# A rebuilt instruction order for a two-kind attention kernel: measured durations of the residual sums and of dependent ScalarE waits put into the planner

## The chip, the cores and the metric

The kernel runs on one core of a Trainium2 chip. The metric is the device time of one execution in microseconds (us), a median over several executions. "DVE" is VectorE, "ACT" ScalarE, "PE" TensorE, "SP" the SyncE sequencer that issues the DMAs.

## The reference

Four layers in a row on x of shape 1 x 2048 x 512 in bf16, with 32 heads of 16 columns: A, B, A, B. Cut to what matters:

```python
def _A_ref(x, wqkv, w_phi, wo):        # linear attention with softmax features
    q, k, v = heads(x @ wqkv)
    phi_q = concat(softmax(q @ w_phi), softmax(-(q @ w_phi)))
    phi_k = concat(softmax(k @ w_phi), softmax(-(k @ w_phi)))
    kv = einsum("bhsf,bhsd->bhfd", phi_k, v)          # a sum over the whole sequence
    z  = einsum("bhsf->bhf", phi_k)
    return (phi_q @ kv) / (phi_q @ z + 1e-6)  @ wo
def _B_ref(x, wqkv, wo):               # sliding window: 8 positions, 2 apart
    ...                                # softmax(q . k[s - 2w]) @ v[s - 2w], then @ wo
for L in range(2):
    x = x + _A_ref(layernorm(x), ...)
    x = x + _B_ref(layernorm(x), ...)
```

The sequence is cut into four blocks of 512 positions. The sums `kv` of a layer A need all four blocks: behind them stands a joint where nothing of that layer's second half can have begun. In what follows joint 0 and joint 1 are the two moments at which the masking operation on the transposed sums (output tile ZM) starts on DVE.

## The kernel before

Each piece of work is a closure in a thread (stage and engine). One string gives the order in which the threads are stepped, one gives each free choice DVE or ACT, one gives buffers. The instructions of every engine, SP included, are issued in the order of the string.

```python
def flex(self, stage, fn, *args):                 # work that DVE or ACT may do
    k = self.nflex; self.nflex += 1
    self.step(stage, "F%d%s" % (k, fn.__name__), fn, *args, _CHOICE[k] == "1")
def run(self):
    self.setup(); self.stages()
    for w in _ORDER.split():                      # 1452 entries
        key = self.names[int(w, 36)]
        i = n.get(key, 0); n[key] = i + 1
        self.threads[key][i]()
```

In layer B the values are copied to 32 partitions for each of four shifts: `vrep`, four DMAs of 131.5 KB each, from the tile V into the tile Vg.

```python
def rdb(s):                                       # "broadcast reload"
    T["P", s] = pr = self.med([4, NB, P], "Prho")
    a = rd[0:1, s, 0:P]
    src = bass.AP(a.tensor, a.offset, [[2 * pitch, 8], [0, 16], [1, 16 * P]])
    nc.sync.dma_start(out=pr[:]..., in_=src)      # DRAM -> SBUF, rows of 4096 bytes
def muld(s):
    nc.vector.tensor_tensor(out=ev[:], in0=ev[:], in1=T["P", s][:], op=ALU.mult)
def vrep(dl):                                     # "value loads"
    ...
    for g in (0, 2, 1, 3):
        a = T["V"][dl:dl + 1, 0:1, 2 + 2 * g:3 + 2 * g]
        src = bass.AP(a.tensor, a.offset, [[4 * a.ap[0][0], H], [1, VGW]])
        nc.sync.dma_start(out=self.Vg[L, b][dl // 2][32 * g:32 * g + 32, dl % 2, 0:VGW], in_=src)
                                                  # SBUF -> SBUF, rows of 4208 bytes
```

## Time and profile before

| | before |
|---|---|
| time, median of 3 | 328.98 us (328.91 to 330.25) |
| span in the profile | 327.5 us |
| busy PE / DVE / ACT | 310.3 / 302.2 / 279.3 us |
| joint 0, joint 1 | 53.70, 209.28 us |
| joint 0 to joint 1 | 155.58 us |
| joint 1 to the end of the last DVE instruction | 113.63 us |
| from there to the end of the span | 4.59 us |

The last three lines are differences of the two joints, of the end of the last DVE instruction (322.91 us) and of the span.

The granted clock is the share of its full speed at which PE was allowed to run.

### The profile page before, as it was taken

What the parts mean: (1) busy time and instruction counts of PE and PEld (TensorE: products, weight loads), DVE (VectorE), ACT (ScalarE), POOL (GpSimd) and SP (SyncE); (2) the same over time, 40 slices, a digit from 0 to 9 for tenths busy, and PEclk for the clock granted to TensorE, in tenths of its full rate; (3) what the DMA queues carried; (4) which work ended last, traced back from release to release, by engine and by line L of the source; (5) the groups of instructions that cost most, each with busy time, mean ns of one, the idle gap of its engine ahead of it and who ended that gap; (6) DMA issues with size and microseconds to landing.
All of it is one profiled execution on the core that took longest, in us unless ns stands there. A gap on an engine that the chain in (4) does not pass through costs nothing. (4 is left out here: it accounts for less than half of the span.)

```text
span 327.5 us, 8033 instructions
## 1 busy us (share of the span) xinstructions
PE 310.3 (95%) x3176; PEld 149.5 (46%) x3203; DVE 302.2 (92%) x439; ACT 279.3 (85%) x634; POOL 25.3 (8%) x50
## 2 busy tenths in 40 slices
PE   7999999999999999999999999979999999999873
PEld 3655456445444444443444455644544454433221
DVE  7998995998998999899999999699999999999993
ACT  5999988998888999989999999798999996676550
POOL 4000000000021003000000000000000208400000
PEclk9999999999999999999999999999999999999999
DMA  7980000004556899998750300023436977679952
GB/s 197 380 197 3 0 2 4 2 20 120 105 148 135 152 164 133 139 121 154 137 135 1 67 3 2 4 59 90 128 58 125 179 146 134 150 139 158 166 176 92
DMA packets 37388, 35.41 MB, mean 108 GB/s; under 512 B 23008, under 2 KB 32224, under 8 KB 37344
## 3 DMA queue, kind: packets, MB, share of 16 engines
q1 hardware_dynamic: 36816, 34.81, 53.6%
q8 instruction: 27, 0.44, 0.6%
q14 instruction: 17, 0.14, 0.2%
q10 hardware_dynamic: 528, 0.02, 0.1%
HBM read 10.50 MB, written 2.36 MB: 39 GB/s over the span
## 5 line engine op out<-in xcount | busy, mean ns | idle before, releaser
L927 PE MATMUL ps<-xnT,WB 128*128 128x512 bf16 x384 | 87.6, 380 | 0.5 <-DMA xnT<-xn 0.5
L1081 DVE TENSOR_TENSOR pav<-PT,Vg 128x4096 bf16<-128x4096 bf16 (+1 forms) x34 | 72.0, 2162 | 1.5 <-DMA Vg<-V 1.0
L1019 DVE TENSOR_TENSOR prod<-QT,K 128x4096 bf16<-128x4096 bf16 x32 | 72.5, 2291 | 0.3 <-ACT QT L192 0.2
L927 PEld LDWEIGHTS <-WB 128*128 128x128 bf16 x384 | 42.3, 114 | 43.3 <-issue 5.8
L520 PEld LDWEIGHTS <-oT 128*128 128x128 bf16 x256 | 23.8, 97 | 34.5 <-ACT oT L192 5.7
L192 ACT CAST oT<-ps 128x512 bf16<-128x512 f32 (+1 forms) x60 | 32.1, 587 | 8.4 <-PE ps L1090 7.1
L706 ACT ACTIVATE Eq<-ps 128x512 bf16<-128x512 f32 x64 | 34.0, 615 | 0.7 <-PE ps L698 0.6
L520 PE MATMUL ps<-WoB,oT 128*128 128x512 bf16 x122 | 32.1, 380 | 2.4 <-ACT oT L192 2.0
L599 ACT ACTIVATE Ek<-ps 128x512 bf16<-128x512 f32 x64 | 33.6, 622 | 0.4 <-PE ps L593 0.2
L698 PE MATMUL ps<-xnT,WA 128*128 128x512 bf16 x128 | 30.7, 380 | 0.6 <-DVE Eq L816 0.6
L540 ACT ACTIVATE sqd<-x 128x512 bf16<-128x512 bf16 x48 | 30.1, 643 | 1.0 <-DVE x L533 0.8
L605 PE MATMUL ps<-WA,xnT 128*128 128x512 bf16 x120 | 30.0, 380 | 0.5 <-issue 0.2
L593 PE MATMUL ps<-WA,xnT 128*128 128x512 bf16 x124 | 29.7, 380 | 0.6 <-DMA xnT<-xn 0.2
L520 PE MATMUL ps<-WoA,oT 128*128 128x512 bf16 x120 | 29.2, 380 | 0.4
L533 DVE SCALAR_TENSOR_TENSOR x<-ps,x 128x512 bf16<-128x512 f32 x38 | 25.4, 686 | 1.9 <-PE ps L520 1.7
L192 ACT CAST V<-ps 128x512 bf16<-128x512 f32 x31 | 17.5, 595 | 4.4 <-PE ps L927 4.3
L192 ACT CAST K<-ps 128x512 bf16<-128x512 f32 x31 | 17.8, 585 | 3.7 <-PE ps L927 3.3
L530 ACT ACTIVATE x<-ps 128x512 bf16<-128x512 f32 x26 | 15.1, 598 | 6.4 <-PE ps L523 6.3
L192 ACT CAST QT<-ps 128x512 bf16<-128x512 f32 x29 | 17.1, 592 | 2.5 <-PE ps L927 2.5
L651 DVE TENSOR_TENSOR Ek<-Ek,rk 128x4096 bf16<-128x4096 bf16 (+1 forms) x10 | 18.6, 1858 | 0.5 <-ACT rk L646 0.5
L593 PEld LDWEIGHTS <-xnT 128*128 128x128 bf16 x128 | 12.1, 97 | 15.4 <-DMA xnT<-xn 0.7
L446 ACT ACTIVATE xn<-x,nmr,rstd 128x512 bf16<-128x512 bf16 x23 | 18.2, 822 | 1.0 <-DVE nmr L435 0.8
(129 smaller groups left out, 433.3 us busy)
## 6 DMA issues: line engine op xcount, KB each, us to landing
Vg<-V SPq DMA_DIRECT2D x128, 131.5 KB, 4.4
Prho<-rd SPq DMA_DIRECT2D x8, 512.0 KB
x<-in_A_x_dram SPq DMA_DIRECT2D x3, 512.0 KB
WB<-in_B_wqkv_dram SPq DMA_DIRECT2D x3, 512.0 KB, 11.6
wraw<-in_A_wqkv_dram SPq DMA_DIRECT2D x4, 256.0 KB, 4.5
out_dram<-x SPq DMA_DIRECT2D x4, 256.0 KB, 2.2
out_dram<-x SPq DMA_DIRECT2D x8, 128.0 KB, 2.2
x<-in_A_x_dram SPq DMA_DIRECT2D x4, 128.0 KB
```

What stands on the lines that cost most here:

```text
L192: self.nc.scalar.copy(out=out, in_=in_)
L520: nc.tensor.matmul(y[:], lhsT=oT[:, c, t * P:(t + 1) * P], rhs=Wo()[:, c, :], start=(c == 0), stop=(c == NB - 1 and not onpe))
L533: nc.vector.scalar_tensor_tensor(out=xb[:, t, :], in0=T[t][:], scalar=1.0, in1=xb[:, t, :], op0=ALU.mult, op1=ALU.add, **kw)
L540: nc.scalar.activation(out=sqd[:], in_=xb[:, t, :], func=ACT.Square, accum_out=T["ss"][:, t:t + 1])
L593: nc.tensor.matmul(pk[:], lhsT=xnT[:, t, k, :], rhs=self.WA[:, k, D:2 * D], start=(k == 0), stop=(k == NB - 1))
L599: nc.scalar.activation(out=T["E"][:, t, s, :], in_=T["k", t][:], func=ACT.Exp, scale=1.0 - 2.0 * s)
L605: nc.tensor.matmul(pv[:], lhsT=xnT[:, t, k, :], rhs=self.WA[:, k, 2 * D:3 * D], start=(k == 0), stop=(k == NB - 1))
L698: nc.tensor.matmul(pq[:], lhsT=self.WA[:, k, hb * P:(hb + 1) * P], rhs=xnT[:, :, k, :], start=(k == 0), stop=(k == NB - 1))
L706: nc.scalar.activation(out=self.Eq[L, b][s][:, :, hb, :], in_=T[hb][:].rearrange("p (t i) -> p t i", t=4), func=ACT.Exp, scale=1.0 - 2.0 * s)
L927: nc.tensor.matmul(pp[:], lhsT=self.WB[:, k, i * D + c:(i + 1) * D:NB], rhs=xnT[:, :, k, :], start=(k == 0), stop=(k == NB - 1))
L1019: nc.vector.tensor_tensor(out=pr[:], in0=QT[:, c:c + 1, :].to_broadcast([P, NW, TB]), in1=win, op=ALU.mult)
L1081: nc.vector.tensor_tensor(out=pv, in0=PT[:, :, lo:lo + n].unsqueeze(1).to_broadcast([P, NB, 2, n]), in1=vw, op=ALU.mult)
```

## The change

The planner that made the order string had its durations of residual sums on DVE and of waits between dependent ACT instructions replaced by measured ones, and built all strings anew: 1452 order entries, 383 choices (68 flipped), all buffer slots. Nothing is computed otherwise; options that were switched off are deleted.

```diff
-    "half_k": ((0, 3), (1, 3)),
+    "half_k": {(0, 3): 1, (1, 3): 1},        # the same two halves for the same two blocks
-    "v_dram": (),                            # was off
-    "rho_pad": 0,                            # was off
 _ORDER = """                                 # 1452 entries, cut
-...
+...
 _CHOICE = (                                  # the first of four lines
-    "0011111111111001110111111010000010010000000000000001011111101100100000110101000110000010000001110111"
+    "1111111111110110111111111010000000001000000001000101001011100100000000110011100010000000000010110100"
 ...
 _SLOTS = {                                   # cut
```

Decoded, the part of the order string that came to matter is that of SP in the first pair of layers (block number in brackets):

```
before: rdb 1 (3) | vrep 0 (0), vrep 0 (1) | tr (2) | vrep 1, 2, 3 (1) | tr (3) | vrep 1, 2, 3 (0)
after:  rdb 1 (3) | vrep 0, 1 (0) | tr (2) | vrep 0, 1, 2, 3 (1)       | tr (3) | vrep 2, 3 (0)
```

## The prediction

> **What bounds the kernel now.** I read four views in this order: busy time by engine, the timeline of slices, a table of windows cut at the two layer joints and at the tail, and the chain of waits. First the page's busy line and its slices.
>
> ```profile
> PE 310.3 (95%) x3176; PEld 149.5 (46%) x3203; DVE 302.2 (92%) x439; ACT 279.3 (85%) x634; POOL 25.3 (8%) x50
> PE   7999999999999999999999999979999999999873
> DVE  7998995998998999899999999699999999999993
> ACT  5999988998888999989999999798999996676550
> ```
>
> Three engines are nearly full at once. TensorE is idle for 327.5 - 310.3 = 17.2 us, VectorE for 25.3, ScalarE for 48.2. A new order does not shorten any instruction; it can only close idle time, so these are all there is to win. VectorE shows two dips, at slice 7 and at slice 26: the joints where the key-value sums of the first-kind layer are complete, are transposed and masked (I call them joint 0, at 53.7 us, and joint 1, at 209.28 us) and everything behind them must start anew. The windows, cut there and where the last VectorE products begin:
>
> ```profile
> 0.00:53.70 53.70, 51.62 (x588) 28.70 (x594) 47.73 (x105) 47.08 (x99) 5.12 (x30) 1.00 0.41 119
> 53.70:209.28 155.58, 152.88 (x1597) 72.89 (x1609) 145.28 (x202) 144.44 (x337) 7.27 (x11) 1.00 0.53 92
> 209.28:240.00 30.72, 28.34 (x424) 14.51 (x428) 28.03 (x69) 27.58 (x75) 0.00 (x0) 1.00 0.27 74
> 240.00:295.12 55.12, 53.95 (x396) 25.26 (x396) 54.34 (x40) 46.15 (x97) 12.91 (x9) 1.00 0.76 139
> 295.12:322.91 27.79, 23.50 (x175) 8.12 (x177) 26.81 (x27) 14.06 (x30) 0.00 (x0) 1.00 0.81 161
> 322.91:327.50 4.59, 0.00 (x0) 0.00 (x0) 0.00 (x0) 0.00 (x0) 0.00 (x0) 0.88 0.22 70
> ```
>
> The columns are the window, its length, then busy time of PE, weight loads, DVE, ACT and POOL, then the granted clock, the DMA share and GB/s. Idle per window, PE / DVE: 2.1 / 6.0 up to joint 0; 2.7 / 10.3 between the joints; 2.4 / 2.7 behind joint 1; 1.2 / 0.8 from 240 to 295; 4.3 / 1.0 in the tail; then 4.6 us in which nothing computes and the last store lands. So TensorE is the bound between the joints (98% busy), and VectorE is the bound from joint 1 to the end: 109.18 us of its work in 113.63 us. The clock is full, so nothing is lost there.
>
> The chain of waits agrees where it can be followed (it breaks off at 219 us): long PE stretches in the projection, then PE waiting for a VectorE product, then short hops.
>
> ```profile
> 266.65 7.77 PE ps L927 x36
> ...
> 292.91 2.30 DVE prod L1019
> 295.21 0.04 issue
> 295.25 0.61 PE ps L1026 x8
> ...
> 315.27 1.00 PE ps L1090 x16
> 316.27 0.00 issue
> 316.28 1.58 ACT oT L192 x3
> 317.86 0.05 issue
> 317.90 0.39 PE ps L520
> ```
>
> 36 matmuls in 7.77 us is 0.216 us each: at full stream. At 295.25 TensorE waits 1.2 us (its largest wait after the start) for the last product; behind that it feeds on what VectorE hands out.
>
> [...]the 384 projection matmuls of L927 have a mean duration of 380 ns but cover 87.6 us together, and 384 x 0.216 = 82.9 us; so 4.7 us of small stalls hide inside "busy". [...]2.29 us for 4096 bf16 elements of SBUF, 0.68 us for 512 of PSUM. So moving small work between engines is an exchange of known prices. [...]behind joint 1 the logarithm of a small tile and the exponential that reads its result start 0.43 us apart (211.00 and 211.43), the full length of the first; the next instruction, which depends on neither, starts 0.21 us after (211.64).
>
> **The change part by part.** The half_k table says the same as before (two halves for the same two blocks), and the DRAM route and pad that are deleted were switched off. Left are three strings: the order, the engine choices and the buffer slots. The lists have equal length (1452 order entries, 383 choices), so every result is computed as before.
>
> Choices: 68 of 383 flip, and they nearly cancel. Prices are mean durations from the groups by form.
> - Layer-norm applications: net 7 go to VectorE (3 in the first norm, 4 behind the first-kind layers), 4 leave it behind the second-kind layers: net +3 x 0.408 = +1.22 us VectorE, -3 x 0.822 = -2.47 ScalarE.
> - PSUM copies of 512 columns: net +1 to VectorE, plus one of 256 columns (taken as 0.42): +0.69 + 0.42; ScalarE -0.59 - 0.37. One weight copy of 1024 columns goes the other way: -0.69 and +1.01.
> - Residual sums: net 2 leave VectorE, one with its accumulator read (0.686 + 0.083) and one without: -1.46; ScalarE +0.598 + 0.204 + 0.598 = +1.40, and TensorE must add x by two more identity matmuls: +2 x 0.216 = +0.43.
> - The broadcast products: 25 direct ones become 23; each change saves VectorE 0.682 - 0.416 = 0.27 and costs a ScalarE copy of 0.589: -0.53 and +1.18.
> Sum: VectorE -0.35, ScalarE +0.16, TensorE +0.43 us. Nothing here is worth a tenth of a per cent. Behind joint 1, where VectorE is the bound, I counted the same list: -0.07 us. So the VectorE-bound last third keeps its 109 us of work; it can gain only from its 4.45 us of idle time.
>
> Order: joint 0 stands behind the same TensorE entry, joint 1 too, and from the third product of block 2 in the last layer on, the next 18 VectorE entries (products and weighted values, some 34 us of work) are the same in both. Changed in detail: the copy at joint 0 goes from VectorE (0.69) to ScalarE (0.59), 0.1 us on a serial path; at joint 1 one query projection moves between the denominators, so that TensorE has work while the reciprocal is made; five instead of three broadcast products there go through a ScalarE copy, which frees PSUM sooner; in the tail, the last copy goes to VectorE and one residual to ScalarE, which puts three instead of four 0.69 us sums behind the last product but adds a 0.42 us copy ahead of them.
>
> What each stretch may give, as a judgement: about a third of its bound engine's idle time, since both orders are products of the same kind of search and much of the idle time is the shape of the graph.
> - up to joint 0: PE idle 2.1, of which 1.27 precedes the first matmul: 0.4 us;
> - between the joints: PE idle 2.7 and perhaps 2.5 of the hidden stalls: 1.6 us;
> - joint 1 to 240 us: VectorE idle 2.7: 0.9 us;
> - from there to the end: VectorE idle 1.8: 0.5 us; the landing of the last store stays.
> That is 3.4, less about 0.2 for the extra matmuls (half of 0.43, as one falls in the tail where TensorE has room): 3.2 us. 328.98 - 3.2 = 325.8 us.
>
> **The rivals.**
> - Full benefit. If the better prices let the order fit the chip, most idle time goes. The floor for TensorE is 310.3 + 0.43 + 1.27 of start + 5.3 behind its last matmul = 317.3 us of span. Getting half way there from 327.5 gives 322.4, a little over 323 us timed. For it: dependent ScalarE pairs are many (some 50 logarithm-exponential pairs) and the old order may have counted them short. Against: ScalarE has 48 us to spare, so its error was mostly absorbed.
> - No benefit. The waits only change places: TensorE between the joints is at 98%, VectorE behind joint 1 at 96%. Then the time is 328 to 329 us.
> - A new wait. In the new order of the DMA queue the first store of block 0's result stands between the value loads of blocks 3 and 2 of the last layer; before, all value loads came first. If the residual is late, the queue holds those loads, and VectorE waits as it did once before (1.0 us at 135.51, for a value load). With rotated buffers and some TensorE waits for PSUM this could cost 1 to 2 us: 330 to 331. Against: the blocked block is the last one used, many products later.
>
> **Range and chances.** The middle estimate is 325.8 us. The third I assumed could be a tenth (328) or two thirds (322.5). The range of 322.4 to 328.7 us should hold it 8 times in 10. Faster by over 2% needs less than 322.4 us, that is 6.6 of about 10 recoverable us: 0.09. Slower by over 2% means 335.6 or more, for which no work was added: 0.02. Within 2%: 0.89.
>
> **What would show it.** Busy time of all three engines should move by less than 1 us each; if VectorE falls by several, my price list is wrong. VectorE's idle time should shrink from 25.3 to 21 to 23 us, TensorE's from 17.2 to about 13 to 15. Joint 1 should come near 207.5 us instead of 209.28, and the stretch from it to the last VectorE instruction should be near 112.3 instead of 113.6. If joint 1 comes at the same time and the gain is all behind it, the step on the TensorE-bound middle was wrong; if a wait for a value load or for PSUM over 1 us appears in VectorE's or TensorE's waits, the third rival is at work. The prediction fails if the time is outside the range, above all if one of the joints turns out to have been a stall of several us that the windows hide.

The 2.29 and 0.68 us are the two-tensor products of DVE in the trace of before (L1019, both operands in SBUF; L816, one in PSUM). The logarithm that starts at 211.00 us lasts 0.40 us there.

## More of the kernel before

In blocks 2 and 3 of layer A the factor rho (one over the denominator) is written to DRAM and read back to be spread over partitions: `rdb`, twice per block, 512 KB each, into tile Prho. `muld` multiplies by it on DVE.

`tr` transposes the normed input of the next layer (xnT).

The prediction shows the busy lines and a table of windows. One line of the page that it does not show is the clock granted to PE in 40 slices, in tenths:

```profile
PEclk9999999999999999999999999999999999999999
```

A 9 is 90% or more, so no slice lost a tenth of it. The trace has one stretch at half clock, from 326.42 us on, behind the end of compute.

## The result, and the profile after

The changed kernel takes 334.37 us (median of 4, 333.08 to 334.77) against 328.95 us for the kernel before in the same series. The ratio is 1.0151, with a 95% interval of 1.0112 to 1.0190. Such a ratio here is always the mean time of one kernel's fast runs over that of the other's of the same rounds, so it is not quite the ratio of the medians. In the whole study one run was slow (336.90 us, of e8_before_value_traffic); it is left out of the ratios. The change is within 2%, but on the other side of 1 than predicted, and outside the range.

These lines are from the changed kernel's page: busy time, then the slices of PE, of DVE and of the granted clock.

```profile
PE 313.4 (94%) x3179; PEld 150.2 (45%) x3205; DVE 302.0 (91%) x440; ACT 280.0 (84%) x635; POOL 21.2 (6%) x50
PE   8999999999997999999999999979999999999782
DVE  8899995998968799999999999698999999999992
PEclk9999999999997999999999999997999999999998
```

DVE and ACT do the same work as before; PE has 3.1 us more, though only three matmul records more. DVE has a new 6 in slice 12 (91.5 to 99.8 us), PE a 7 in slice 13, and the clock, without a dip before, has a 7 in slice 13 and one in slice 28. The table of windows of the changed kernel, cut at its own joints and at the places that answer to those of before (columns: window, length, busy PE, weight loads, DVE, ACT, POOL, granted clock, DMA share, GB/s):

```profile
54.53:212.77 158.24, 154.07 (x1598) 73.63 (x1609) 144.44 (x200) 145.97 (x340) 6.53 (x12) 0.99 0.50 90
212.77:240.00 27.23, 24.34 (x402) 11.71 (x406) 23.98 (x56) 23.59 (x59) 0.00 (x0) 0.94 0.31 83
240.00:298.58 58.58, 58.42 (x408) 27.98 (x412) 57.81 (x53) 49.95 (x113) 9.54 (x9) 1.00 0.73 127
327.44:332.69 5.25, 0.00 (x0) 0.00 (x0) 0.00 (x0) 0.00 (x0) 0.00 (x0) 0.83 0.27 87
```

So the span grew by 5.2 us in four places: joint 0 comes 0.83 later (54.53 for 53.70), the stretch between the joints is 2.66 longer (158.24 for 155.58), the one behind joint 1 is 1.04 longer (327.44 - 212.77 = 114.67 for 113.63), and the end without compute 0.66 (5.25 for 4.59). Joint 0 needs no cause in the order: the later profiles with full clock at the start have it at 53.41 to 54.61 with the changed beginning and at 53.80 to 54.70 with the old one. The other three differences repeat.

**The new wait at 100 us.** The timeline of the kernel before, SP's DMA issues (columns: start, us from first to last issue of the group, what, count):

```profile
87.06 3.03 SPq L451 DMA_TRANSPOSE xnT<-xn  x1
90.19 0.60 SPq L831 DMA_DIRECT2D Prho<-rd  x1
95.28 6.79 SPq L988 DMA_DIRECT2D Vg<-V  x8
```

and of the kernel after:

```profile
86.67 2.87 SPq L448 DMA_TRANSPOSE xnT<-xn  x1
90.10 0.59 SPq L828 DMA_DIRECT2D Prho<-rd  x1
90.80 9.96 SPq L976 DMA_DIRECT2D Vg<-V  x8
102.76 2.42 SPq L448 DMA_TRANSPOSE xnT<-xn  x1
```

The second reload of block 3 is issued at the same time in both. Before, the next eight DMAs (value loads) follow at 95.28, when it is nearly through. In the new order ACT makes V of block 0 earlier (its last copy ends at 87.73 us instead of 95.20), so SP need not wait for it, and they stand right behind the reload, at 90.80. The old order kept the two apart only by chance: its loads waited for V, which came when the reload was nearly through. The DMA records of the trace show what this does to the reload's 4096-byte packets (counted per us, with the mean time of one):

```
            before                    after
93 us   28 of 277 ns              18 of 471 ns  and 16 value packets of 398 ns
94 us   30 of 281 ns              17 of 501 ns  and 16 value packets of 491 ns
95 us   the last 10, of 261 ns    16 of 535 ns  and 16 value packets of 508 ns
97 us   -                         16 of 498 ns  and 16 value packets of 516 ns
98 us   -                         the last 2
```

About half as many packets, each about twice as long (471 to 535 ns for 261 to 281), and from 92 to 97 us the DMA share of the windows view is 1.04 of the core's 16 engines where it was 0.41. The product that needs the reload, in the timeline of the kernel before:

```profile
96.03 2.39 DVE L835 TENSOR_TENSOR Eq<-Eq,Prho 128x2048 bf16<-128x2048 bf16 x2
100.14 0.65 PE L900 MATMUL ps<-Eq,R 32*32 32x512 bf16 x32
```

and after (in square brackets: idle time just before, and what ended it):

```profile
98.59 0.43 PE L897 MATMUL ps<-Eq,R 32*32 32x512 bf16 x16
100.30 1.23 DVE L832 TENSOR_TENSOR Eq<-Eq,Prho 128x2048 bf16<-128x2048 bf16 x1 [2.91 <-DMA Prho<-rd]
101.58 0.44 PE L897 MATMUL ps<-Eq,R 32*32 32x512 bf16 x16 [2.55 <-DVE Eq L832]
```

DVE waits 2.91 us for the reload, and PE, which holds the second half of the matmuls that read Eq at the head of its queue, 2.55 us for DVE.

**The half clock.** From 102.24 us, PE runs for 3.41 us at half clock. In the windows view of the changed kernel the second line has the granted clock 0.61 (third number from the end):

```profile
98.00:101.58 3.58, 1.03 (x21) 0.26 (x19) 1.28 (x2) 0.97 (x3) 0.00 (x0) 1.00 0.54 108
101.58:106.00 4.42, 4.42 (x27) 1.72 (x27) 4.38 (x6) 3.72 (x7) 0.29 (x1) 0.61 0.78 150
```

In that stretch, matmuls of 512 columns start 0.427 us apart, for 0.216 us elsewhere. The three half-clock stretches of this execution start at 102.24, 225.12 and 330.93 us, the first two last 3.413 us each, and the later two start 122.88 and 228.69 us behind the first: 36 and 67 times 3.4133 us. The two starts ahead of the end of compute lie 36 such lengths apart in after_again too (100.2 and 223.1 us) and 26 in e4_block1_first (224.1 and 312.8). In the 3.41 us ahead of the first stretch PE was busy for 0.25 of the time (0.86 us), ahead of the second for 0.64 (2.17 us). That share alone does not tell: from 310.46 to 313.87 us PE was busy for 0.46 of the time, and the clock stayed at 1.00 behind it. These shares take PE's busy time from the trace, whose matmul ends are modelled. The second stretch lies behind joint 1; there PE does many small matmuls of 32 rows or columns between waits of 0.2 to 0.6 us. The third lies behind the end of compute and costs nothing.

**The end.** The last DVE instruction and the last four stores in the timeline of the kernel before:

```profile
322.22 0.69 DVE L533 SCALAR_TENSOR_TENSOR x<-ps,x 128x512 bf16<-128x512 f32 x1 [0.35 <-PE ps L520]
320.62 3.10 SPq L544 DMA_DIRECT2D out_dram<-x  x4
```

and after:

```profile
326.75 0.69 DVE L530 SCALAR_TENSOR_TENSOR x<-ps,x 128x512 bf16<-128x512 f32 x1 [0.43 <-PE ps L517]
325.74 3.54 SPq L541 DMA_DIRECT2D out_dram<-x  x4
```

The issue of the last store is through at 323.72 before, 0.81 us behind the end of that DVE instruction, and at 329.28 after, 1.84 us behind it. In the new order the last store but one, which stores a residual made on ACT, is in issue from 327.23 to 328.81 us, and the last store stands behind it; before, the last store but one took 0.33 us. This repeats: 0.79 to 1.60 us in the seven other executions with the new second part, 0.33 us in all six with the old one.

### The profile page after: what moved, and what is told of

It is laid out like the page before. It is cut to its first block, busy times and chain, and to the rows that moved or that the text cites. A ratio compares the mean times of both kernels' runs of the same rounds, so it can differ in the third digit from the quotient of the medians.

```text
span 332.7 us, 8019 instructions
## 1 busy us (share of the span) xinstructions
PE 313.4 (94%) x3179; PEld 150.2 (45%) x3205; DVE 302.0 (91%) x440; ACT 280.0 (84%) x635; POOL 21.2 (6%) x50
## 4 chain that ended last, share of the span: by engine, by line
PE 74%; ACT 10%; DMA 9%; DVE 4%; issue 1%; SPq 1%; DVEq 0%; ACTq 0%
PE ps L924 24%; PE ps L517 12%; PE ps L590 7%; PE ps L602 7%; DMA Vg<-V 6%; PE ps L695 5%; PE ps L1012 4%; PE ps L1076 4%; ACT Eq L703 3%; DMA Prho<-rd 3%; PE ps L665 2%; PE ps L285 2%; PE ps L457 1%; DVE pav L1067 1%; PE ps L897 1%
## 5 line engine op out<-in xcount | busy, mean ns | idle before, releaser
L924 PE MATMUL ps<-xnT,WB 128*128 128x512 bf16 x384 | 89.0, 385 | 0.0
L190 ACT CAST oT<-ps 128x512 bf16<-128x512 f32 (+1 forms) x56 | 30.0, 585 | 8.5 <-PE ps L1076 6.5
L517 PE MATMUL ps<-WoA,oT 128*128 128x512 bf16 x120 | 31.4, 392 | 0.6 <-DVE oT L188 0.2
L590 PE MATMUL ps<-WA,xnT 128*128 128x512 bf16 x123 | 29.3, 379 | 0.5 <-issue 0.2
L602 PE MATMUL ps<-WA,xnT 128*128 128x512 bf16 x122 | 29.4, 379 | 0.2
L530 DVE SCALAR_TENSOR_TENSOR x<-ps,x 128x512 bf16<-128x512 f32 x36 | 23.6, 685 | 3.3 <-PE ps L517 3.2
L527 ACT ACTIVATE x<-ps 128x512 bf16<-128x512 f32 x28 | 16.5, 600 | 9.3 <-PE ps L520 9.2
L1076 PE MATMUL ps<-pav,indAV 128*32 128x512 bf16 (+1 forms) x272 | 17.9, 370 | 3.3 <-DVE pav L1067 3.3
L602 PEld LDWEIGHTS <-xnT 128*128 128x128 bf16 x128 | 12.3, 98 | 14.6 <-issue 0.4
L590 PEld LDWEIGHTS <-xnT 128*128 128x128 bf16 x128 | 12.2, 98 | 14.9 <-issue 0.8
```

The lines of the kernel that those rows point to most:

```text
L190: self.nc.scalar.copy(out=out, in_=in_)
L517: nc.tensor.matmul(y[:], lhsT=oT[:, c, t * P:(t + 1) * P], rhs=Wo()[:, c, :], start=(c == 0), stop=(c == NB - 1 and not onpe))
L590: nc.tensor.matmul(pk[:], lhsT=xnT[:, t, k, :], rhs=self.WA[:, k, D:2 * D], start=(k == 0), stop=(k == NB - 1))
L602: nc.tensor.matmul(pv[:], lhsT=xnT[:, t, k, :], rhs=self.WA[:, k, 2 * D:3 * D], start=(k == 0), stop=(k == NB - 1))
L924: nc.tensor.matmul(pp[:], lhsT=self.WB[:, k, i * D + c:(i + 1) * D:NB], rhs=xnT[:, :, k, :], start=(k == 0), stop=(k == NB - 1))
L1076: nc.tensor.matmul(po[32 * c:32 * c + 32, lo:lo + n], lhsT=self.indAV[:], rhs=T["p", q][:, c, hf, lo:lo + n], start=(hf == 0), stop=(hf == ...
```

## The experiments

Theory: the value loads right behind the reload slow it; DVE and PE wait for it; the wait brings the half clock; behind joint 1 a second half-clock window falls. Rivals: the new order is slower as such; or the queue is merely too full there, and any repair moves the wait; or the time comes from the second half. Twelve runs were made, in three batches, each beside the kernel before on the same chip (medians 329.49, 329.88 and 329.75 us, seven runs each). All gave correct results. The table gathers what all of them left (the median of e8_before_value_traffic counts its slow run; its three fast ones took 331.03 to 332.85 us); stretches and windows are of the one profiled execution.

| run | batch | median us (runs) | ratio, 95% interval | joint 0 to 1 | joint 1 to last DVE | half clock from, us (before the end of compute) |
|---|---|---|---|---|---|---|
| before | - | 328.95 | 1 | 155.58 | 113.63 | none |
| after | - | 334.37 (4) | 1.0151, 1.0112 to 1.0190 | 158.24 | 114.67 | 102.2, 225.1 |
| h_before_then_after | 1 | 330.92 (4) | 1.0057, 1.0020 to 1.0093 | 155.67 | 113.04 | none |
| h_after_then_before | 1 | 333.24 (6) | 1.0115, 1.0096 to 1.0134 | 157.88 | 113.65 | 100.4 |
| e1_loads_later | 1 | 334.33 (4) | 1.0170, 1.0124 to 1.0217 | 160.05 | 112.99 | 124.2 |
| e3_fill | 1 | 332.07 (4) | 1.0087, 1.0058 to 1.0117 | 156.72 | 112.97 | none |
| after_again | 2 | 333.15 (4) | 1.0093, 1.0067 to 1.0120 | 158.11 | 114.60 | 100.2, 223.1 |
| e4_block1_first | 2 | 334.56 (4) | 1.0126, 1.0073 to 1.0179 | 158.42 | 114.67 | 224.1, 312.8 |
| e5_fixed_then_before | 2 | 333.93 (4) | 1.0126, 1.0097 to 1.0156 | 159.61 | 113.62 | none |
| e6_before_traffic | 2 | 329.11 (4) | 0.9976, 0.9955 to 0.9996 | 155.38 | 113.62 | none |
| e8_before_value_traffic | 3 | 332.58 (4) | 1.0059, 1.0031 to 1.0087 | 158.41 | 113.62 | none |
| e9_hold | 3 | 328.86 (5) | 0.9973, 0.9957 to 0.9990 | 154.60 | 112.98 | 10.9 |
| e10_hold_then_before | 3 | 328.70 (4) | 0.9966, 0.9944 to 0.9989 | 154.02 | 113.72 | none |
| e11_hold_fill | 3 | 329.33 (4) | 0.9989, 0.9972 to 1.0006 | 153.78 | 113.93 | none |

### Which half of the program loses: two crosses

The entries of one kernel up to joint 1 (its transposing step), then the rest in the order of the other, choices likewise; buffers renamed where the two meet.

```diff
-_ORDER, _CHOICE, _SLOTS of one kernel
+_ORDER = order_A up to ('akv1', 'tr') + entries of order_B not yet taken
+_CHOICE of A for those entries, of B for the rest
```

> Order, choices and slots of the kernel before up to joint 1 and of the changed kernel from there on. Theory: joint 1 near 209.3 us, a half-clock window behind it, time 330.2 to 331 us. Rival (nothing is lost behind joint 1): 328.6 to 329.3 us. Rival (the new order behind joint 1 is a gain): under 328.3 us.

> Order, choices and slots of the changed kernel up to joint 1 and of the kernel before from there on. Theory (about 3.5 us are lost ahead of joint 1 and about 1.5 behind it, in a second half-clock window): joint 1 at 212.5 to 213 us, no half-clock window near 225 us, time 332.3 to 333.3 us. Rival (all is lost ahead of joint 1): 334 to 334.8 us. Rival (the new order behind joint 1 is a gain that the first loss hides): over 335 us.

The changed first part brings 157.88 us between the joints with the old second part, the old first part 155.67 with the new second part: the loss between the joints belongs to the first part. The new second part took 113.04 us at full clock, 0.6 less than the old one's 113.63; in the changed kernel, with a half-clock window in it, 114.67. So up to the last DVE instruction the new order is a little quicker behind joint 1. The longer end (5.28 us for 4.55 in the profile of before) takes this back, and in the changed kernel the half clock is a loss on top. The timed runs of this cross were 0.57% slower than before; two of the four had a mean clock of 0.986 and 0.992 against 0.995 to 0.999 for before. But the two at full clock (330.25 and 330.41 us) were above the median of before (329.49) too, and its one profile does not show the half-clock window that its theory forecast. In that profile joint 0 comes 1.00 us later than in that of before, with the same beginning. So the clock as the reason for its time is not shown.

### The changed kernel once more

> The changed kernel unaltered, as the control on the chip on which the next ones run. Both theories: 334 to 335.5 us, half-clock windows near 102 us and in some runs near 225 us.

The same strings, on another chip: DVE waits 3.11 us for the reload at 99.38, half-clock windows at 100.2 and 223.1, between the joints 158.11. The pattern repeats, though the time, 333.15 us, is below the 334 to 335.5 expected; the ratio was 1.0093 where the first series had 1.0151. The size of the loss differs from series to series by half a per cent, so the stretches of the profile, which agree within 0.2 us, carry the argument below.

### What the clock costs: TensorE kept busy in the wait

```diff
+            if (L, b) == (0, 3):       # in mo, ahead of the matmuls that wait for the product
+                for _ in range(10):
+                    nc.tensor.matmul(T[3][:], lhsT=self.ident[:], rhs=self.WA[:, 0, 0:TB], start=True, stop=True)
```

The ten matmuls have no use; the real ones overwrite their result.

> The changed kernel with ten idle matmuls of 128x128x512 ahead of block 3's output products, into a PSUM bank that these then overwrite; they run while TensorE would wait for the late reload. Theory (the stall costs twice: the wait itself and then a 3.41 us window at half clock): VectorE's 2.9 us wait stays, the half-clock window near 102 us is gone, and the time is 332.3 to 333.2 us, 1.2 to 2 us under the changed kernel. Rival (VectorE is the bound there and the clock does not matter): 334.2 to 334.8 us. Rival (the fillers delay real work): over 335 us.

The wait for the reload stays, in the timeline of this kernel:

```profile
98.53 2.32 PE L898 MATMUL ps<-WA,ident 128*128 128x512 bf16 x10
100.50 1.23 DVE L834 TENSOR_TENSOR Eq<-Eq,Prho 128x2048 bf16<-128x2048 bf16 x1 [3.07 <-DMA Prho<-rd]
101.78 0.44 PE L902 MATMUL ps<-Eq,R 32*32 32x512 bf16 x16 [0.56 <-DVE Eq L834]
```

but no half-clock window follows, and the stretch is 156.72 us, 1.4 less than the 158.1 of the two unchanged profiles (158.24, 158.11). In the windows view, which rounds its length differently:

```profile
54.57:211.28 156.71, 155.33 (x1621) 74.26 (x1619) 144.24 (x199) 145.65 (x340) 6.60 (x12) 1.00 0.56 91
```

So the clock is about 1.4 us of the loss, by one profile of this kernel, and the wait by itself another part. The median time, 332.07 us, is just under the 332.3 to 333.2 expected; two of the four runs had a mean clock of 0.991.

### Two repairs that moved the wait

First, the value loads of block 0 were put behind the next transposing DMA:

```diff
 SP: rdb 1 (3)
-    vrep 0, 1 (0) | tr (2)
+    tr (2) | vrep 0, 1 (0)
     vrep 0, 1, 2, 3 (1) | tr (3) | vrep 2, 3 (0)
```

> The changed kernel with one edit in the DMA queue's order: the first two groups of value loads of block 0 (eight DMAs, 1 MB) go behind the transposing DMA of block 2's normalised rows instead of ahead of it. Theory (the value loads share the DMA engines with the second broadcast reload of block 3 and delay its landing): the reload's 4096-byte packets fall from about 500 to about 250 ns, VectorE's 2.9 us wait and TensorE's 2.6 us wait at 100 us vanish, no half-clock window starts near 102 us, joint 1 comes near 208.6 instead of 212.8 us, time 329.8 to 330.6 us. Rival (the reload is late because it is issued late, and the load order does not matter): VectorE still waits over 2 us there, time 334 to 334.8 us. Rival (the loads are now late themselves): a wait for a value load over 1 us appears behind 110 us and the time stays over 332 us.

The reload was quick again (265 to 280 ns per packet) and the wait at 100 us gone. But now twenty-four value loads, eight of block 0 and then sixteen of block 1, stood in one row from 100.70 us, and block 1's, which are used first, came last. DVE's waits in this kernel (total, times, longest):

```profile
DVE pav L1069 <- DMA Vg<-V: 6.3, 4, 2.5
```

PE then waited 3.35 us at 123.19 and had its half clock from 124.2. The stretch was 160.05 us, longer than without the repair: its third rival was right.

Second, the loads were split, so that block 1 kept its place:

```diff
 SP: rdb 1 (3)
-    vrep 0, 1 (0) | tr (2) | vrep 0, 1, 2, 3 (1) | tr (3)
+    tr (2) | vrep 0 (0) | vrep 0, 1, 2, 3 (1) | vrep 1 (0) | tr (3)
```

once with the changed second part, once with the old one behind joint 1.

> The changed kernel with two edits in the DMA queue's order: of block 0's value loads, the first group goes behind the transposing DMA of block 2, the second behind all of block 1's (block 1 is used first). Theory (the late reload is the loss; the previous try lost it again only because block 1's loads then stood behind eight DMAs of block 0): the reload's packets near 260 ns, no wait over 1 us of VectorE for a DMA between 95 and 140 us, no half-clock window ahead of joint 1, joint 1 near 208 to 209.5 us, time 329.3 to 331 us. Rival (the order between the joints is worse in itself, and without one wait another takes its place): joint 1 still at 211 us or later, time over 332.5 us.

> The same up to joint 1, and the kernel before from joint 1 on. Theory (nothing else is lost ahead of joint 1; behind it both orders take the same time at full clock, and the new one falls to half clock in some runs): 328.5 to 329.8 us, within 0.3% of the kernel before. Rival (the new order's first stretch, mended, is a gain of over 1 us that could be kept): under 328.3 us.

Neither got better. The waits of DVE with the changed second part:

```profile
DVE x L532 <- PE ps L519: 3.7, 4, 1.6
DVE pav L1069 <- DMA Vg<-V: 2.8, 3, 1.4
```

Value loads came late again (1.41 us at 120.89), and the transposing DMA made PE (1.91 us at 129.71) and through it a residual sum wait (1.52 us at 133.82). Its issue began at 121.83 us, about when it does in the changed kernel (121.55), but lasted 5.51 us instead of 2.82, behind a row of twenty-four loads instead of sixteen. Between the joints 158.42 and 159.61. In both, DMAs in the queue between 95 and 135 us came too late. These two misses left a question: was the collision at 91 us the cause at all, or just one face of a queue with no room?

### Does traffic behind the reload slow it? Two trials in the kernel before

Eight DMAs with no use, of about the value loads' size, right behind the second reload of block 3. First from SBUF to DRAM:

```diff
             nc.sync.dma_start(out=pr[:]..., in_=src)
+            if (L, b, s) == (0, 3, 1):
+                junk = self.dram.tile([8, 32, 2104], BF16, name="junk")
+                for g in range(8):
+                    nc.sync.dma_start(out=junk[g], in_=self.WA[32 * (g % 4):32 * (g % 4) + 32, ...])
```

> The kernel before with eight DMAs of 135 KB from constant SBUF tiles to an unused DRAM tile, issued right behind the second broadcast reload of block 3 in the same queue; nothing waits for them. Theory (traffic behind the reload is enough to delay it): the reload's 4096-byte packets rise from about 250 to about 450 ns, VectorE waits 1.5 to 3.5 us for it near 97 us, time 331 to 334 us, more if TensorE falls to half clock behind the wait. Rival (a DMA issued later does not slow an earlier one, the changed kernel's reload was late for another reason): no new wait, 329 to 330 us.

No new wait came. The dummy DMAs ran beside the reload (SP's timeline of this kernel):

```profile
90.32 0.60 SPq L833 DMA_DIRECT2D Prho<-rd  x1
90.97 5.86 SPq L837 DMA_DIRECT2D junk<-WA  x8
```

and the trace has 27 to 39 reload packets per us at 218 to 279 ns from 92 to 95 us, beside 14 to 32 dummy packets. The time was 0.9976 of before (0.9955 to 0.9996). As nothing in this kernel can make it quicker, this also shows that a ratio of 0.997 or 0.998 need not be a gain. The theory as it stood then, that any traffic behind the reload slows it, was wrong. Then traffic of the value loads' own kind:

```diff
+            if (L, b, s) == (0, 3, 1):
+                junk = self.bigp.tile([P, 2, NB * KVW], BF16, name="junk", tag="big3")   # free at that time
+                for dl in range(2):
+                    for g in (0, 2, 1, 3):
+                        a = self.WA[dl:dl + 1, 0:1, 2 + 2 * g:3 + 2 * g]
+                        src = bass.AP(a.tensor, a.offset, [[4 * a.ap[0][0], H], [1, VGW]])
+                        nc.sync.dma_start(out=junk[32 * g:32 * g + 32, dl, 0:VGW], in_=src)
```

> The kernel before plus eight dummy loads right behind the second broadcast reload, this time of the value loads' own kind (from every fourth partition of one tile in SBUF to 32 partitions of another, 4208 bytes a row), where the earlier trial wrote from SBUF to DRAM and changed nothing. Theory[...]: the reload's 4096-byte packets go from 220 to 280 ns to 450 to 540 ns, it lands 2 to 3 us later, VectorE waits 1.5 to 3 us for it near 97 to 100 us, the stretch from joint 0 to joint 1 goes from 155.5 to 157 to 159, ratio 1.004 to 1.012. Rival (traffic behind the reload is not what slows it): packets under 300 ns, no wait for it, ratio within 0.3 per cent of 1.

Now the kernel before shows the fault: 14 to 18 reload packets per us at 484 to 506 ns from 94 to 97 us, and in its timeline

```profile
99.80 1.22 DVE L844 TENSOR_TENSOR Eq<-Eq,Prho 128x2048 bf16<-128x2048 bf16 x1 [2.14 <-DMA Prho<-rd]
```

The stretch is 158.41 us instead of 155.58, the ratio 1.0059. Part of that is not the reload: the real value loads were pushed back too, and DVE waits 2.2 us at 138.71 for one. So it shows that this kind of traffic slows the reload, by as much as in the changed kernel; it is no measure of what that alone costs. It also has no half-clock window though DVE waited: in the old order PE has other matmuls to do then (its longest gap from 90 to 110 us is 0.90 us, at 93.98, for another DMA), where in the new order the matmuls that need the product are next in its queue. Which difference between the two trials counts stays open: the dummy DMAs differ in where they write (DRAM or SBUF) and in what they read (32 neighbouring partitions or every fourth). It is not that two transfers shared a fixed rate. At 93 us the first trial moved 27 reload and 32 dummy packets in one us, 245 KB; at 96 us the second moved 16 and 16, 133 KB. In both the times of the packets add up to 15.6 or 15.7 us, about all that 16 DMA engines have in one us.

### The start of the loads held back

The repair that puts nothing behind the transposing DMA: a tiny DMA ahead of the eight value loads, which reads a result that is ready when the reload is nearly through, so that SP waits there.

```diff
 SP: rdb 1 (3)
-    vrep 0, 1 (0) | tr (2) | ...
+    hold, vrep 0, 1 (0) | tr (2) | ...        # emitted behind the last residual of block 2
+            if (L, b, dl) == (0, 0, 0):
+                hold = self.dram.tile([1, 64], BF16, name="hold")
+                nc.sync.dma_start(out=hold[:], in_=self.x[2][0:1, 3, 0:64])
```

It ran with the changed second part, with the old second part, and with six useless matmuls in the first block's mixing step behind joint 1.

> The changed kernel; the only edit: the first eight value loads of block 0 stand behind a tiny DMA that reads a result of the third block's output projection, which is ready near 95 us, so they start when they start in the kernel before, and not right behind the second broadcast reload (90.8 us). Unlike the two earlier attempts nothing is put behind the next transposing DMA, so the loads of block 1 are not later. Theory (the reload shares the queue with the value loads and lands late, and the half-clock window follows from the wait): the reload's 4096-byte packets are back at 220 to 285 ns, VectorE's wait for the reload at 100 us is gone (under 0.4), no half-clock window near 102, and the stretch from joint 0 to joint 1 falls from 158.1 to 155.3 to 156.3 us; the ratio to the kernel before is 0.998 to 1.006. Rival (the queue between 95 and 135 us is simply tighter in this order, whatever the start): the wait goes, another appears for value loads, stretch over 157.5, ratio still over 1.008.

> The held order up to joint 1, the order and choices of the kernel before from there on. Theory: behind joint 1 both orders take 118.1 to 118.5 us at full clock and differ only when a half-clock window falls there; so this equals the held kernel within 0.3 per cent where that has no such window, and is 1 to 1.7 us quicker where it has. Ratio to before 0.997 to 1.004. Rival (the end of the changed order is slower by itself): 0.4 per cent or more between this and the held kernel with no half-clock window in either.

> The held kernel plus six 512-column matmuls with no use in the first block's mixing step right behind joint 1, where the small matmuls of that step stand between short waits ahead of the half-clock window at 225 us. Theory[...]: no half-clock window between joint 1 and the end of the work in any profile, joint 1 to end 118.0 to 118.8 us, mean clock over 0.990 in the timed runs, and the time at or below the held kernel's. Rival (the fill costs more than the clock gives[...]): joint 1 to end 119 or more.

All three stretches (154.60, 154.02, 153.78 us) are below the 155.3 to 156.3 expected of the first. The first took 328.86 us, 0.9973 of before (0.9957 to 0.9990); the second 328.70 us, 0.9966 (0.9944 to 0.9989). This shows that the loss is gone. That these kernels are quicker than the kernel before is not shown by the ratios, since the trial with dummy DMAs came to 0.9976; for a gain there are only the stretches. SP's timeline of the second:

```profile
90.14 0.59 SPq L830 DMA_DIRECT2D Prho<-rd  x1
94.92 0.26 SPq L973 DMA_DIRECT2D hold<-x  x1
95.28 5.03 SPq L981 DMA_DIRECT2D Vg<-V  x8
100.42 3.18 SPq L450 DMA_TRANSPOSE xnT<-xn  x1
```

the product, in its timeline:

```profile
97.81 1.23 DVE L834 TENSOR_TENSOR Eq<-Eq,Prho 128x2048 bf16<-128x2048 bf16 x1 [0.38 <-DMA Prho<-rd]
```

and its two stretches in the windows view:

```profile
54.58:208.60 154.02, 153.17 (x1611) 73.27 (x1609) 144.26 (x200) 145.66 (x340) 6.61 (x12) 1.00 0.53 93
208.60:322.32 113.72, 106.58 (x1001) 47.83 (x1001) 109.20 (x133) 87.87 (x200) 15.07 (x9) 1.00 0.65 127
```

Reload packets are back at 251 to 279 ns. PE is idle for 154.02 - 153.17 = 0.85 us between the joints, where the kernel before has 2.70 and the changed one 158.24 - 154.07 = 4.17. The transposing DMA starts at 100.42 instead of 102.76. In the first held run DVE still waited 0.97 us for the reload, more than the 0.4 expected; in that execution everything was 2 us late, after a half-clock window at 10.9 us in the opening, and the transposing DMA ahead of the reload landed at 94.67.

With the old second part the ratio is 0.07 percentage points lower, far less than the intervals are wide: as expected, the two second parts do not differ measurably at full clock. The new one is 0.74 us shorter to the last DVE instruction (112.98 for 113.72) and loses as much at the end (329.7 - 324.07 = 5.6 us of stores for 327.1 - 322.32 = 4.8). The useless matmuls behind joint 1 did not pay: joint 1 to the last DVE instruction 113.93 us, 0.95 more than without them, and to the end of the span 119.2, where 118.0 to 118.8 was expected. There was no half-clock window for them to prevent in that execution, nor in the held one. Their rival was right.

## Why the prediction was wrong

**Busy time and price list.** Right for DVE and ACT, which moved by -0.2 and +0.7 us, within the 1 us it allowed. PE moved by 3.1, but this need not be more work: 2 x 3.41 us at half clock can make its work last up to 3.4 us longer. And the measure itself varies: the trial with dummy DMAs, with the order of before, has 312.0 us of busy PE for 310.3. The idle time did not shrink to 21 to 23 us on DVE; it grew from 25.3 to 332.7 - 302.0 = 30.7, and joint 1 came at 212.77 instead of 207.5.

**"What each stretch may give ... about a third of its bound engine's idle time".** This is the step that failed, in its entry "between the joints ... 1.6 us": it came as 2.66 us of loss. The entry's mechanism and size were not far off, though. With the loads held, the new order needs 154.60, 154.02 and 153.78 us (mean 154.1) where the old one needs 155.58, 155.38 and 155.67 (mean 155.5): 1.4 us gained, mostly PE's idle time, as it said. That its 1.6 came so near is partly luck. It counted on 2.5 us of "hidden stalls" in the projection matmuls, which are hardly there: the 384 matmuls come in 26 unbroken rows, and starts further apart than 0.23 us inside these rows add only 0.43 us to the busy time. The rest of the 4.7 us is the modelled end of each row's last matmul, 26 x (0.380 - 0.216) = 4.3 us. What it left out is that the same order starts eight value loads into a running reload. The loss can be split by the profiles: 155.5 - 1.4 (order) + 2.6 (the wait; 156.7 in the run with the fill, less 154.1) + 1.4 (half clock; 158.1 less 156.7) = 158.1 us. Each term is the difference of two runs, so the sum comes out by construction: it is a split and no check.

**"Joint 1 to 240 us: 0.9 us" and "to the end: 0.5 us".** Together 1.4 us. At full clock the stretch from joint 1 to the last DVE instruction is 112.97 to 113.04 us in the four profiles of the new second part without a half-clock window or a fill, 0.6 less than 113.63, and the end behind it is 0.6 to 1.0 longer than the 4.6 of before (5.1 to 5.6). So nothing is left of it. In the changed kernel the half-clock window adds 1.7 us (114.67 less 112.98).

**"The clock is full, so nothing is lost there."** True of the kernel before, and taken as true of the changed one without a word. It was not among the rivals, and it is some 3 us of the changed kernel's profile: 1.4 between the joints, 1.7 behind joint 1.

**The third rival, "a new wait" from the order of the DMA queue.** Right in kind and in its sign (a wait over 1 us that DVE shows for a DMA), wrong in place and form. It looked for a blocked queue in the last layer, priced at 1 to 2 us. What came was two DMAs slowing each other in the first pair of layers. The prediction named a wait "for a value load or for PSUM" as its sign; what was waited for was the reload, and the value loads were the ones in its way. **The first two rivals**: far from the full benefit. Between the joints the order gains 1.4 us once the loads are held; over the whole kernel this cannot be told from nil (spans of 327.1 and 327.6 us in the two held profiles without a half-clock window in the opening, for 327.5 before).

Open: what makes one kind of DMA slow the reload and another not; how much of the gain is the flipped choices and how much the order, as no run separates them; and how often a timed run has its half-clock windows in a costly place. The mean clock alone does not tell: one run of the held kernel took 328.97 us at a mean clock of 0.986.

## What to carry to other kernels

When an instruction order is rebuilt, compare the DMA queue too: a transfer that becomes ready sooner may start into one that is needed sooner, and a planner that gives every DMA a fixed duration would not see it (how this planner prices DMAs is not on record). Putting it behind the next transfer just moved the wait here; holding it until the urgent one was through, in place, turned a kernel of 1.009 to 1.015 of the time into one of 0.997, about level with before. The price depended on the kind of both transfers: the reload's 4096-byte packets took 261 to 281 ns alone (the kernel before, 93 to 95 us), 218 to 279 ns beside SBUF-to-DRAM traffic (e6_before_traffic) and 471 to 535 ns beside SBUF-to-SBUF value loads (the changed kernel, 93 to 97 us). And price a new PE stall at more than its length: in all four executions in which PE waited 2.55 us or more in one piece between the joints (2.55 us in after, 2.76 in after_again, 2.59 in h_after_then_before, 3.35 in e1_loads_later), half clock came with it, and in none of the other ten was there half clock between the joints.
